# Attention and two MLPs on one core: four splits of weight sums moved into the first MLP's last block, eight moved inside their groups, ScalarE copies put behind the first product's copy

## The chip, the core and the metric

The kernel runs on one core of a Trainium2 chip. The metric is the device time of one execution in microseconds (us); lower is better. The core has a matrix engine (TensorE, PE in the profile; PEld is its loading of weights), VectorE (DVE), ScalarE (ACT), GpSimd (POOL) and SyncE (SP), which here issues all the DMA transfers. Each engine works through its own instructions in order and waits for others by semaphores. Matmuls write to PSUM banks; a bank that is read by DVE or ACT can be written again only when the read is done.

## What is computed

Windowed attention with a linear bias, then a first MLP (2304 tokens, 512 to 2048 to 512), then a second, gated MLP (512 to 1536 to 512) on normed input. In full float32; the kernel makes each float32 product of three passes over a "high" part and a "low" part (x = high + low, both in the matrix engine's reduced float32 format): high*high, high*low, low*high.

```python
def _moe_ref(x, w_in, w_out):
    h = x @ w_in
    relu6 = np.clip(h + 3.0, 0.0, 6.0)
    g = h * relu6 / 6.0
    return (g @ w_out).astype(np.float32)

def _moe2_ref(x, w_gate, w_val, w_out, rms_g):
    rms = np.sqrt(np.mean(x * x, axis=-1, keepdims=True) + 1e-06)
    xn = x / rms * rms_g
    g = xn @ w_gate
    silu = g * (1.0 / (1.0 + np.exp(-g)))
    val = xn @ w_val
    return (silu * val @ w_out).astype(np.float32)

def reference(**kwargs):            # attention, then both MLPs on [tokens, 512]
    ...
    x = _moe_ref(x=x, **moe_kwargs)
    return _moe2_ref(x=x, **moe2_kwargs)
```

## The kernel before

**First MLP.** It goes over blocks of 384 tokens (3 tiles of 128), 16 steps m of 128 hidden columns each. A step is `product1` (12 matmuls into the one bank `ps_h`, L577), a chain on ACT and DVE that makes the activation and its high and low part (L816 on ACT, L817 on DVE, L822 on ACT, L828 on DVE), and `product2` of the step before (9 matmuls, L590). Beside it run the attention of later blocks and the conversion of the second MLP's weights from 64-bit words. The conversion also writes, for each pair of steps, float32 sums of parts of the output weights to DRAM (`sum32`). In the last block, at 463 to 532 us, DVE scales the first pair's input (L736, step 2), makes sums of it, and ACT and DVE split them.

**Second MLP.** It runs in three pairs of blocks (768 tokens), 12 steps each, so in 36 groups i = 0 to 35, pair s = i // 12. A group makes gate and value by a Strassen-Winograd scheme: seven products of 6 matmuls each (products 0 to 6, L942) instead of eight. Three PSUM banks serve a group, the next group has three others. The order by hand is, in `group`: jobs called "start"; product 0 into `ps_1`; ACT copies it to `s1` (L950); product 1 into `ps_6`; DVE adds `s1` and `ps_6` to u[:,0] (L953), which frees `ps_6` for product 3; product 2 adds into `ps_1`, so it waits until L950 has read that bank; ACT makes the first silu (L956); jobs "silu"; product 3 into `ps_6`; DVE adds `s1` and `ps_6` to u[:,1] (L959), which frees `ps_6` for product 5; jobs "sum"; product 4 into `ps_5`; DVE adds (L962), which frees `ps_5` for product 6; product 5; DVE adds (L964); second silu (L965); jobs "silu 2"; product 6; DVE adds and multiplies (L968, L969); jobs "end".

For s = 0 the output product is `outputs`, every second group, from 36 matmuls (L992) whose results DVE adds up (L999). For s = 1 and 2 it is made in rounds of four groups, again by a Winograd scheme: class `Round` with seven units (c, g, a, b, e, f, d) of two halves each, whose 6 matmuls (L1116) run behind the groups i0 + 5, i0 + 6 and i0 + 7 (`phase`). DVE adds their results up (L1147), or ACT copies the first (L1145). The seven operands of a round (B22, B11, B21, T3, T1, T2, T4, halves 0 and 1) are made by jobs: "sum" is a DVE difference (L1090), "high" an ACT copy (L1093), "low" a DVE subtraction (L1096). `ROUND_JOBS` says where: the key (-1, "start") is the start of group i0 + 3, (0, "start") that of group i0 + 4, and so on; numbers stand for the positions in `phase` or `outputs`. The first round starts at group 12, so its (0, ...) jobs lie in group 16, and those of the later rounds in 20, 24, 28 and 32; the last round has its own list, `FINAL_JOBS`.

**Splits of the weights' sums.** The rounds read four of the seven weight operands from sums that must be split into high and low part first: 12 splits, `load_sum` (one DMA of 256 KB from `sum32` into the tile `ws`) and `split_sum` (ACT copies the high part, L320; DVE subtracts, L321; two DMAs store them). `SPLIT_AT` puts split k's load at the start of one group and the split itself behind the first silu ("silu") of the next; the twelve lie in groups 7, 8, 9, 10 and 12 to 19. In the order on DVE that is ahead of L959.

**Input of a pair.** `turn(s)` lays out the jobs for the next pair's input: a load of 1.5 MB (`x.load`), scaling, sums (L742 to L748), high parts (L766) and low parts (L770) of the seven Winograd operands.

Of the kernel before, what the change touches and what calls it, by code (L numbers as in the profile page):

```python
# [10 lines left out]
F32 = mybir.dt.float32  # L11
# [9 lines left out]
P = 128  # L21
# [3 lines left out]
DM = H * D  # L25
# [44 lines left out]
ADDED_TO = {"c": "C12", "a": "V", "g": "C22", "b": "C11", "e": "V", "f": "V", "d": "Z"}  # L70
SUMMED = ["C11", "C12", "C22", "V", "Z"]
BLOCK_RING = (12, 10, 11)
SPLIT_AT = (7, 8, 9, 10, 12, 13, 14, 15, 16, 17, 18, 19)
OPERANDS = "B22 B11 B21 T3 T1 T2 T4".split()
CHAINED = {"b": "a", "d": "e"}
ROUND_JOBS = {
# [2 lines left out]
    (-1, 2): [("high", "B11", 0)],  # L79
    (-1, 3): [("low", "B11", 0)],  # L80
    (-1, 4): [("sum", "T1", 0)],
    (-1, 5): [("sum", "T3", 0), ("high", "T3", 0)],
    (0, "start"): [("high", "B11", 1), ("high", "B22", 1), ("sum", "T2", 0)],
    (0, "silu"): [("low", "B11", 1), ("sum", "T1", 1), ("low", "B22", 1)],
    (0, "silu 2"): [("sum", "T3", 1), ("high", "T3", 1)],
    (0, "end"): [("low", "T3", 0)],
    (1, "start"): [("sum", "T2", 1), ("high", "B21", 0), ("high", "B21", 1)],
    (1, "silu"): [("low", "T3", 1), ("low", "B21", 0)],
    (1, "silu 2"): [("low", "B21", 1)],
    (1, "end"): [("sum", "T4", 0)],  # L90
    (1, 0): [("sum", "T4", 1)],
    (1, 2): [("high", "T1", 0), ("high", "T1", 1)],
    (1, 3): [("low", "T1", 0)],
    (2, "start"): [("low", "T1", 1), ("high", "T2", 0), ("high", "T2", 1)],
    (2, "silu"): [("low", "T2", 0), ("low", "T2", 1)],
    (2, 3): [("high", "T4", 0), ("high", "T4", 1)],
    (3, "start"): [("low", "T4", 0), ("low", "T4", 1)],
# [36 lines left out]
def fused_kernel(ctx: ExitStack, tc: tile.TileContext, qd, kd, v, w1, w2, rms_g, out, out_t):  # L134
# [113 lines left out]
    class Second:  # L248
# [57 lines left out]
                    self.x = []  # L306
                    self.begin()

        def load_sum(self, i):
            k = i % 2  # L310
            if k not in self.late:
                self.late[k] = tuple(
                    ypool.tile([P, DM], F32, tag=tag, name=name, bufs=1 if tag == "yt" else 3)
                    for tag, name in (("y", "ws"), ("yt" if k else "y", "wt"))
                )
            sp.dma_start(out=self.late[k][0], in_=self.sum32[i // 2][:, k])
# [460 lines left out]
    for p, (b, m0, m1) in enumerate(PARTS):  # L777
# [14 lines left out]
        for m in range(m0, m1):  # L792
# [68 lines left out]
            if last:  # L861
                if m == 1:
                    fed = Inputs(0)
                    fed.load()
                elif m == 2:
                    for c in range(KC):
                        fed.scale(c, vec)
                for x in early:
                    k = m - EARLY[x.m]
                    if k == 0:  # L870
                        x.load()
                    elif k == 1:
                        x.sums()
                    if k in (3, 4):
                        x.high(k - 3)
                    if k in (4, 5):
                        x.low(k - 4)
                if m == M1 - 1:
                    x.low(1)
                    parts[4].load()  # L880
                if m in FIRST_SUMS:
                    fed.sum(FIRST_SUMS[m], vec, temps.tile([P, 2, 3 * P], F32, tag="r", name="sum"))
                if m in FIRST_OPS:
                    fed.high(GROUP.index(FIRST_OPS[m]))
                    fed.low(GROUP.index(FIRST_OPS[m]))
# [4 lines left out]
    n = 3 * P  # L890
# [18 lines left out]
    def settle(which):  # L909

        for x in waiting:
            if which in x:
                x.pop(which)()
        waiting[:] = [x for x in waiting if x]
# [3 lines left out]
    def job(i, at, f, *args):  # L918
        jobs.setdefault((i, at), []).append((f, args))
# [5 lines left out]
    def group(i):  # L925
# [23 lines left out]
        product(0, ps_1)  # L949
        act.copy(s1, ps_1)  # L950
        settle("high")
        product(1, ps_6)
        vec.tensor_add(u[:, 0], s1, ps_6)  # L953
        settle("low")
# [88 lines left out]
    def total(name, d):  # L1043

        k = 5 * d + SUMMED.index(name)
        if k < 5:
            return words_of(SUMS[0], k, (1,))[:, 0]
        return words_of(BLOCK_RING[k - 5], 4, (1,))[:, 0] if k < 8 else left(F32)[:, k - 8]

    class Round:  # L1050
# [82 lines left out]
        def phase(self, off, by):  # L1133
            own = [(ps_out, "o2"), (ps_a, "T")], [banks[(by + 1) % 2][2], banks[(by + 1) % 2][1]]
            for j, (k, d) in enumerate(UNITS[off]):
                d = int(d)
                if k in CHAINED:
                    ps = self.ps[CHAINED[k], d]
                else:
                    p, tag = own[k in "gf"][d]  # L1140
                    ps = self.ps[k, d] = p.tile([P, 4 * P], F32, tag=tag, name="ps_y")[:, :n]
                self.unit(k, d, ps)
                to = total(ADDED_TO[k], d)
                if self.q == 0 and k not in "ef":
                    act.copy(to, ps)  # L1145
                else:
                    vec.tensor_add(to, to, ps)  # L1147
                if d:
                    i = 7 * self.r + self.order().index(k) + 3
                    if i // 7 < len(rounds):  # L1150
                        rounds[i // 7].fetch(rounds[i // 7].order()[i % 7])
                do(by, j)
                if self.q == ROUNDS - 1:
                    on = vec if self.final else pool
                    store = lambda name, rows, cols: sp.dma_start(
                        out=out_t[(2 * rows + d) * P : (2 * rows + d + 1) * P, (2 * (self.s - 1) + cols) * n : (2 * (self.s - 1) + cols + 1) * n],
                        in_=total(name, d),
                    )
                    if k == "b":
                        store("C11", 0, 0)  # L1160
                    elif k == "f":
                        for x, cols in (("C12", 1), ("C22", 1)):
                            (pool if x == "C12" else on).tensor_add(total(x, d), total(x, d), total("V", d))  # L1163
                            store(x, x == "C22", cols)
                    elif k == "d":
                        on.tensor_sub(total("Z", d), total("C22", d), total("Z", d))
                        store("Z", 1, 0)

    ROUNDS = M2 // ROUND
    rounds = [Round(s, q) for s in range(1, PAIRS2) for q in range(ROUNDS)]  # L1170
# [17 lines left out]
    def turn(s):  # L1188

        i, x = s * M2, Inputs(s + 1)  # L1190
        job(i + 5, "start", x.load)
        if s:
            for c in range(KC):
                job(i + 6, ("silu", "end")[c // 2], x.scale, c, act)
            job(i + 7, "silu", x.later, "S1", 0)
            job(i + 7, 2, x.later, "S2", 1)
            job(i + 7, 2, x.high, 0)
            job(i + 7, 4, x.low, 0)
            job(i + 9, 3, x.later, "S4", 2)
            job(i + 9, 3, x.high, 1)  # L1200
            job(i + 10, "silu 2", x.low, 1)
            job(i + 10, 3, x.later, "S3", 3)
            for k in range(2, 7):
                job(i + 11, {2: "silu", 3: "sum", 5: "silu 2"}.get(k, "end"), x.high, k)
                job(i + 11, {2: "silu 2", 3: "end"}.get(k, k - 3), x.low, k)
            return
        for c in range(KC):
            job(i + 6, (1, 3)[c // 2], x.scale, c, act)
# [11 lines left out]

    for x in rounds:
        x.plan(job)
    for i, at_ in enumerate(SPLIT_AT):
        job(at_ - 1, "start", W2.load_sum, i)
        job(at_, "silu", W2.split_sum, i)

    for i in range(M2 * PAIRS2):
        s, m = divmod(i, M2)
# [11 lines left out]
            outputs(i - 2, i)  # L1240
        elif i == M2 - 1:
            outputs(i - 3, i)
        if i == M2:
            for k in SEQUENCE[:3]:
                rounds[0].fetch(k)
        x = Round.all.get(i - ROUND)
# [53 lines left out]
```

## Time and profile before

| | |
|---|---|
| time, median of 3 runs | 970.88 us (969.73 to 973.53) |
| the profiled execution's own time | 970.52 us |
| its span in the profile | 968.8 us |
| time outside the span | 1.72 us |
| first MLP's last block | 463 to 532 us |
| second MLP, groups 0 to 35 | 532 to 964 us |

A page of the profile gives busy time and share of each engine. The list of waits says for how long an engine idled in front of a line, in how many places, the longest of them, and whose instruction ended it. A timeline row gives the start, the length of the run of instructions, engine, line, operation, output tile and inputs, shapes, the count, and in brackets the idle time before and what ended it. Times are microseconds from the span's start. The ends of matmuls are modelled; their starts are measured.

### The profile page before, as it was taken

The page shows a single profiled execution, that of the slowest core. Times are in us where ns is not written, and L with a number is a line of the kernel's source. Part 1 is how long each engine was busy: PE and PEld are TensorE (multiplying, and loading weights), DVE is VectorE, ACT ScalarE, POOL GpSimd, SP SyncE. Part 2 cuts the span into 40 slices and gives each one's busy share as a digit, 9 for nine tenths or more (in the row PEclk, how much of TensorE's full clock was granted, in tenths as well). Part 3 has the DMA queues.
Part 4 walks back from the last instruction along what each step waited for, and adds up shares of the span by engine and source line. Part 5 has one row for each costly group of instructions (what it writes and reads, how often), then busy time and mean ns, then how long its engine had stood idle before and what let it go on. Part 6 is the DMA issues. An engine that isn't in the chain of part 4 may idle for free.

```text
span 968.8 us, 15365 instructions
## 1 busy us (share of the span) xinstructions
PE 937.8 (97%) x5408; PEld 840.3 (87%) x5408; DVE 692.6 (71%) x1464; ACT 478.5 (49%) x1049; POOL 217.4 (22%) x359
## 2 busy tenths in 40 slices
PE   7899999999999999999999999999989998999998
PEld 4677888888888888888898999889989898999997
DVE  5788566556788778777567657787575777675778
ACT  6899556355656655654355453433135333223331
POOL 4333013233334424333323323300000000020001
PEclk9999999999999999999999999999999999999999
DMA  7546411113765555553454768775989675786626
GB/s 239 198 162 221 154 39 32 41 52 112 249 227 182 197 188 184 183 175 120 142 206 175 282 251 325 293 302 219 304 323 377 235 249 179 272 286 241 218 88 217
DMA packets 96044, 197.08 MB, mean 203 GB/s; under 512 B 7008, under 2 KB 67424, under 8 KB 92768
## 3 DMA queue, kind: packets, MB, share of 16 engines
q1 hardware_dynamic: 95968, 196.11, 58.2%
q8 instruction: 42, 0.69, 0.3%
q14 instruction: 34, 0.28, 0.1%
HBM read 142.61 MB, written 53.48 MB: 202 GB/s over the span
## 4 chain that ended last, share of the span: by engine, by line
PE 73%; DVE 11%; ACT 7%; DMA 4%; issue 3%; POOL 2%; SPq 0%; ACTq 0%; POOLq 0%; DVEq 0%
PE ps_o L590 18%; PE ps_h L577 18%; PE ps_o L942 8%; PE ps_S L942 6%; PE ps_y L1116 5%; PE ps_A L942 4%; PE ps_y L992 4%; PE ps_h L942 3%; PE ps_av L511 2%; DMA tx<-b 2%; DMA tw<-t 1%; PE ps_t L493 1%; DVE u L1147 1%; ACT t L479 1%; DVE wx L203 1%
## 5 line engine op out<-in xcount | busy, mean ns | idle before, releaser
L590 PE MATMUL ps_o<-w,g 128*128 128x512 f32 x864 | 224.1, 402 | 2.0 <-DVE w L207 1.9
L577 PE MATMUL ps_h<-xs,w 128*128 128x384 f32 x1152 | 220.4, 339 | 0.2 <-DVE t L817 0.2
L577 PEld LDWEIGHTS ps_h<-xs,w 128*128 128x128 f32 x1152 | 202.3, 188 | 6.7 <-DVE t L817 1.0
L590 PEld LDWEIGHTS ps_o<-w,g 128*128 128x128 f32 x864 | 156.1, 188 | 41.1 <-issue 6.1
L817 DVE SCALAR_TENSOR_TENSOR t<-t,ps_h 128x384 f32<-128x384 f32 x96 | 53.0, 553 | 90.5 <-ACT t L816 90.3
L816 ACT ACTIVATE t<-ps_h,three 128x384 f32<-128x384 f32 x96 | 55.3, 576 | 81.3 <-PE ps_h L577 76.0
L1116 PE MATMUL ps_y<-u 128*128 128x384 f32 x432 | 83.8, 335 | 0.2
L1163 POOL TENSOR_TENSOR u<-u 128x384 f32<-128x384 f32 x6 | 7.6, 1287 | 328.5 <-DVE u L1147 328.5
L1116 PEld LDWEIGHTS ps_y<-u 128*128 128x128 f32 x432 | 75.6, 188 | 0.8 <-DVE u L1147 0.4
L479 ACT ACTIVATE t<-t,m 128x128 f32<-128x128 f32 (+1 forms) x144 | 61.2, 426 | 29.4 <-DVE t L471 14.9
L822 ACT CAST g<-t 128x384 fp32r<-128x384 f32 x96 | 49.3, 514 | 52.5 <-DVE t L817 50.7
L965 ACT ACTIVATE r<-r 128x384 f32<-128x384 f32 x36 | 18.9, 526 | 108.3 <-DVE r L964 108.3
L828 DVE TENSOR_TENSOR g<-t,g 128x384 fp32r<-128x384 f32 x96 | 54.8, 571 | 23.1 <-ACT g L822 22.8
L942 PE MATMUL ps_o<-S,tw 128*128 128x384 f32 x336 | 66.7, 340 | 0.3 <-DVE t L962 0.3
L481 POOL TENSOR_SCALAR r<-den 128x2 f32<-128x2 f32 x72 | 27.4, 381 | 172.6 <-ACT t L479 171.0
L942 PEld LDWEIGHTS ps_o<-S,tw 128*128 128x128 f32 x336 | 59.0, 188 | 2.4 <-DVE u L953 1.6
L482 POOL TENSOR_TENSOR r<-r,minus 128x2 f32<-128x2 f32 x72 | 55.9, 776 | 6.0
L500 POOL TENSOR_SCALAR_AFFINE_SELECT pt<-pt 128x256 f32<-128x256 f32 x82 | 36.9, 452 | 81.9 <-ACT pt L498 79.0
L992 PE MATMUL ps_y<-wo,g 128*128 128x512 f32 x216 | 50.3, 391 | 0.0
L1093 ACT CAST u<-u 128x384 fp32r<-128x384 f32 x66 | 31.8, 512 | 36.6 <-DVE u L1090 20.8
L992 PEld LDWEIGHTS ps_y<-wo,g 128*128 128x128 f32 x216 | 40.8, 189 | 8.1
L464 DVE CUSTOM_DVE_ANT_0 t<-ps_s,rel 128x256 f32<-128x256 f32 (+2 forms) x128 | 45.2, 394 | 3.2 <-PE ps_s L450 3.2
(168 smaller groups left out, 1753.7 us busy)
## 6 DMA issues: line engine op xcount, KB each, us to landing
tw<-t SPq DMA_DIRECT2D x52, 896.0 KB, 6.5
wraw<-w SPq DMA_DIRECT2D x36, 512.0 KB, 4.1
wraw<-w SPq DMA_DIRECT2D x16, 1024.0 KB, 8.8
u<-s SPq DMA_DIRECT2D x48, 256.0 KB, 5.9
t<-th SPq DMA_DIRECT2D x12, 896.0 KB, 4.5
t<-tl SPq DMA_DIRECT2D x12, 896.0 KB, 4.4
u<-w SPq DMA_DIRECT2D x36, 256.0 KB, 5.3
w<-w SPq DMA_DIRECT2D x12, 512.0 KB, 2.9
```

Of the source, the lines that this page charges most:

```text
L464: vec.tensor_tensor_reduce(out=self.t[:, a, c0:], in0=s[:, c0:], in1=(rel_split if self.i in SPLITS else rel)[:, c0:], scale=2.0 ** (-8.0 ...
L479: act.activation(p, p, AF.Exp, bias=self.m[:, a : a + 1], scale=-1.0, accum_out=self.den[:, a : a + 1])
L482: pool.tensor_tensor(self.r, self.r, minus, ALU.pow)
L577: pe.matmul(ps[:, : n * P], lhsT=w[:, a, c * P : (c + 1) * P], rhs=xs[c][:, b, : n * P], start=(k == 0), stop=(k == 3 * KC - 1),)
L590: pe.matmul(o, lhsT=g[:, a, i * P : (i + 1) * P], rhs=w[:, b], start=(m == first and a == 0 and b == 0), stop=(m == last and a == 1),)
L816: act.activation(r[:, :nq], ps[:, :nq], AF.Relu, bias=three)
L817: vec.scalar_tensor_tensor(out=r[:, :nq], in0=r[:, :nq], scalar=6.0, in1=ps[:, :nq], op0=ALU.min, op1=ALU.mult)
L822: act.copy(g[:, 0, :nq], r[:, :nq])
L828: vec.tensor_sub(g[:, 1, :nq], r[:, :nq], f32(g[:, 0, :nq]))
L942: pe.matmul(ps, lhsT=w[a][:, k, c * P : (c + 1) * P], rhs=x[:, b, c], start=(start and j == 0), stop=(j == 5), skip_group_check=True,)
L992: pe.matmul(ps, lhsT=gs[i + k][:, a, t // 3, t % 3 * P : (t % 3 + 1) * P], rhs=wo[i + k][:, b], start=(k == 0 and a == 0 and b == 0), stop ...
L1116: pe.matmul(ps, lhsT=w[:, p, a, d * P : (d + 1) * P], rhs=self.part(name, p, b), start=(p == j == 0 and k not in CHAINED), stop=(p == 1 an ...
```

## The change

Four of the twelve splits (0 to 3) are made in steps 0 to 6 of the first MLP's last block, in rooms (tags "A22" and "S3") that the pair's operands use later in that block: load at step 0, 0, 3, 4 and split at the end of step 2, 3, 5, 6. The eight others go to groups 9 and 10 ("silu"), 12 ("silu 2"), 13 ("silu"), 16, 19, 20 and 21 ("sum", which is behind L959). A new position "copied" lies behind the copy of `s1`; the high parts that stood at "start" of the rounds' groups (0), (1) and (2), and the high part of T3, half 0, that stood at the end of the round phase before, go there. For the third pair the input's load is issued at the start of group 14 instead of 17; the low part of operand 1 goes from "silu 2" of group 22 to position 1 of the phase behind that group, and that of operand 6 from position 3 of the phase behind group 23 to "sum" of group 24. The first round's first three weights are fetched behind group 15 instead of 12. The end of `phase` becomes a method `give` with the same sums and stores on the same engines.

```diff
-SPLIT_AT = (7, 8, 9, 10, 12, 13, 14, 15, 16, 17, 18, 19)
+EARLY_SPLITS = {0: ("A22", 0, 2), 1: ("S3", 0, 3), 2: ("A22", 3, 5), 3: ("S3", 4, 6)}
+SPLIT_AT = {4: (9, "silu"), 5: (10, "silu"), 6: (12, "silu 2"), 7: (13, "silu"), 8: (16, "sum"), 9: (19, "sum"), 10: (20, "sum"), 11: (21, "sum")}
...
-    (-1, 5): [("sum", "T3", 0), ("high", "T3", 0)],
-    (0, "start"): [("high", "B11", 1), ("high", "B22", 1), ("sum", "T2", 0)],
+    (-1, 5): [("sum", "T3", 0)],
+    (0, "start"): [("sum", "T2", 0)],
+    (0, "copied"): [("high", "T3", 0), ("high", "B11", 1), ("high", "B22", 1)],
...
-    (1, "start"): [("sum", "T2", 1), ("high", "B21", 0), ("high", "B21", 1)],
+    (1, "start"): [("sum", "T2", 1)],
+    (1, "copied"): [("high", "B21", 0), ("high", "B21", 1)],
...
-    (2, "start"): [("low", "T1", 1), ("high", "T2", 0), ("high", "T2", 1)],
+    (2, "start"): [("low", "T1", 1)],
+    (2, "copied"): [("high", "T2", 0), ("high", "T2", 1)],
...
-        def load_sum(self, i):
+        def load_sum(self, i, tag=None):
             k = i % 2
-            if k not in self.late:
+            if tag:
+                t = opool.tile([P, 3, DM], F32, tag=tag, name="ws")
+                self.late[k] = t[:, 0], t[:, 1]
+            elif i - 2 in EARLY_SPLITS or k not in self.late:
...
+                for i, (tag, load_at, split_at) in EARLY_SPLITS.items():
+                    if m == load_at:
+                        W2.load_sum(i, tag)
+                    if m == split_at:
+                        W2.split_sum(i)
                 if m == M1 - 1:
...
         act.copy(s1, ps_1)
         settle("high")
+        do(i, "copied")
         product(1, ps_6)
...
-        job(i + 5, "start", x.load)
+        job(i + (2 if s else 5), "start", x.load)
...
-            job(i + 10, "silu 2", x.low, 1)
+            job(i + 10, 1, x.low, 1)
...
-                job(i + 11, {2: "silu 2", 3: "end"}.get(k, k - 3), x.low, k)
+                job(i + 11 + (k == 6), {2: "silu 2", 3: "end", 6: "sum"}.get(k, k - 3), x.low, k)
...
-    for i, at_ in enumerate(SPLIT_AT):
-        job(at_ - 1, "start", W2.load_sum, i)
-        job(at_, "silu", W2.split_sum, i)
+    for i, at_ in SPLIT_AT.items():
+        job(at_[0] - 1, "start", W2.load_sum, i)
+        job(*at_, W2.split_sum, i)
...
-        if i == M2:
+        if i == M2 + 3:
             for k in SEQUENCE[:3]:
                 rounds[0].fetch(k)
```

## Rows read from the trace of the kernel before

**Rows 1.** The page, part 1: busy us, share of the span, instructions.

```profile
PE 937.8 (97%) x5408; PEld 840.3 (87%) x5408; DVE 692.6 (71%) x1464; ACT 478.5 (49%) x1049; POOL 217.4 (22%) x359
```

**Rows 2.** PE's waits, whole span: us in total, times, longest us.

```profile
PE ps_h L942 <- ACT s L950: 7.3, 5, 3.1
...
PE ps_A L942 <- DVE u L959: 2.7, 5, 2.0
...
PE ps_o L942 <- DVE u L959: 2.0, 4, 1.0
...
PE ps_y L1116 <- DVE u L1147: 0.4, 1, 0.4
```

**Rows 3.** Timeline of PE in group 24: products 1 to 4.

```profile
808.22 1.22 PE L942 MATMUL ps_A<-S,tw 128*128 128x384 f32 x6
812.52 1.83 PE L942 MATMUL ps_h<-A,tw 128*128 128x384 f32 x6 [3.09 <-ACT s L950]
814.16 2.12 PE L942 MATMUL ps_A<-S,tw 128*128 128x384 f32 x6
816.08 1.42 PE L942 MATMUL ps_S<-S,tw 128*128 128x384 f32 x6
```

**Rows 4.** Timeline of ACT at the start of group 24.

```profile
810.76 0.92 ACT L1093 CAST u<-u 128x384 fp32r<-128x384 f32 x2 [6.99 <-DVE u L1090]
811.59 0.51 ACT L1093 CAST S<-u 128x384 fp32r<-128x384 f32 x1
812.00 0.47 ACT L950 COPY s<-ps_h 128x384 f32<-128x384 f32 x1
```

**Rows 5.** Timeline of DVE at the start of group 24.

```profile
807.85 0.95 DVE L770 TENSOR_TENSOR S<-sums,S 128x768 fp32r<-128x768 f32 x1
...
810.12 1.14 DVE L1090 TENSOR_TENSOR u<-u 128x384 f32<-128x384 f32 x2
812.50 0.55 DVE L953 TENSOR_TENSOR u<-s,ps_A 128x384 f32<-128x384 f32 x1 [1.24 <-ACT s L950]
```

**Rows 6.** Timeline of PE in group 8: product 5, and the outputs behind product 6.

```profile
628.19 0.63 PE L942 MATMUL ps_A<-A,th 128*128 128x384 f32 x2 [2.04 <-DVE u L959]
...
631.74 1.52 PE L992 MATMUL ps_y<-wo,g 128*128 128x512 f32 x5
```

**Rows 7.** Timeline of DVE in group 8: the split's subtraction.

```profile
626.98 0.69 DVE L321 TENSOR_TENSOR ws<-ws,wt 128x512 fp32r<-128x512 f32 x1 [2.23 <-ACT wt L320]
```

**Rows 8.** Timeline of PE in groups 14, 16, 20 and 28.

```profile
700.91 1.32 PE L942 MATMUL ps_A<-A,tw 128*128 128x384 f32 x6 [0.17 <-DVE u L959]
...
711.34 1.20 PE L942 MATMUL ps_h<-A,tw 128*128 128x384 f32 x6
712.38 1.20 PE L942 MATMUL ps_A<-S,tw 128*128 128x384 f32 x6
715.42 1.32 PE L942 MATMUL ps_h<-A,tw 128*128 128x384 f32 x6 [1.84 <-ACT s L950]
...
764.12 1.32 PE L942 MATMUL ps_h<-A,tw 128*128 128x384 f32 x6 [0.92 <-ACT s L950]
...
860.38 1.32 PE L942 MATMUL ps_h<-A,tw 128*128 128x384 f32 x6 [1.31 <-ACT s L950]
```

**Rows 9.** Timeline of DVE in groups 16 and 28: the differences ahead of L953.

```profile
713.08 1.14 DVE L1090 TENSOR_TENSOR u<-u 128x384 f32<-128x384 f32 x2
...
857.62 2.19 DVE L1090 TENSOR_TENSOR u<-u 128x384 f32<-128x384 f32 x2
```

**Rows 10.** Timeline of DVE in the first MLP's last block, steps 2 and 3.

```profile
476.61 3.17 DVE L736 TENSOR_SCALAR x2raw<-x2raw,g_sb 128x768 f32<-128x768 f32 x4
479.70 0.54 DVE L817 SCALAR_TENSOR_TENSOR t<-t,ps_h 128x384 f32<-128x384 f32 x1
```

**Rows 11.** Timeline of PE in the same block: product 1 of step 4.

```profile
480.87 2.35 PE L577 MATMUL ps_h<-xs,w 128*128 128x384 f32 x12
```

**Rows 12.** The tile `ws` (loads, ACT copies' inputs, stores of the splits): its transfers' landing.

```profile
DMA to landing us min/median/max: 2.1/6.3/11.3
```

More of the change, by code (lines that the diff above doesn't have):

```diff
@@ L1152, in phase, with give, store, combine @@
                 do(by, j)
[L1153 to L1167, printed above, removed]
+                if self.q == ROUNDS - 1 and k in "bfd":
+                    self.give(k, d)
+        def give(self, k, d):
+            def store(name, rows, cols):
+                row, col = (2 * rows + d) * P, (2 * (self.s - 1) + cols) * n
+                sp.dma_start(out=out_t[row : row + P, col : col + n], in_=total(name, d))
+            def combine(name):
+                x, on = total(name, d), vec if self.final and name != "C12" else pool
+                if name == "Z":
+                    on.tensor_sub(x, total("C22", d), x)
+                else:
+                    on.tensor_add(x, x, total("V", d))
+                store(name, name != "C12", name != "Z")
+            if k == "b":
+                store("C11", 0, 0)
+            for name in {"b": (), "f": ("C12", "C22"), "d": ("Z",)}[k]:
+                combine(name)
     ROUNDS = M2 // ROUND
```

## The prediction

> **What bounds the kernel now.** I read the busy shares first: TensorE (PE) is busy 937.8 of the span, VectorE (DVE) 71% [rows 1]. So time can only come out of PE's pauses, and the list of PE's waits says who ends them [rows 2]. The large entries of the second MLP are two. Product 2 waits for `s1` (L950, on ScalarE, ACT): 7.3 us in 5 waits. Product 5 waits for L959, the DVE sum that frees `ps_6`: 2.7 and 2.0 us in 9 waits.
>
> An idle figure is less than what a pause costs. In group 16 products 0 and 1 start at 711.34 and 712.38, so six matmuls take about 1.05; product 2 starts at 715.42, 1.99 late, where the row says 1.84 idle, since the end of product 1 is modelled 0.15 behind its pace; product 2 itself shows 1.32 instead of 1.20 [rows 8]. So I price each pause at **its idle figure plus 0.27**.
>
> A long pause costs more. In group 24 product 2 waits 3.09, and the two products that begin behind it take 1.64 and 1.92 from start to start instead of 1.05 [rows 3]: 1.5 more. In group 8 the 12 matmuls from 628.19 to 631.74 take 3.55 instead of 2.10, also 1.5 more, behind a pause of 2.04 [rows 6]. I saw PE at about half its pace nowhere else in the second MLP.
>
> **Why those waits exist.** Engines work in program order. In group 24, `do(i, "start")` puts three ACT copies (810.76 to 812.1) ahead of the copy of `s1` at 812.00 [rows 4]; the first needs a DVE difference that ends DVE's backlog at 811.26 [rows 5]. PE had the input of `s1` ready at 808.2, so nothing but the order holds it. In group 8, the split's subtraction (L321) stands on DVE ahead of L959, and DVE idles 2.23 until ACT has made that split's copy [rows 7].
>
> **The change part by part.**
> *Splits.* The subtraction no longer stands ahead of L959 in groups 7, 8, 14, 15, 18 and, below what the list names, 17 (split gone), 12 (now behind the second silu), 16 and 19 (now behind L959). Of the nine L959 waits I attribute one to group 13, which keeps its split; it is an ordinary one, as that of group 14, 0.17 [rows 8]. Eight go: 4.7 - 0.2 = 4.5 idle, plus 8 x 0.27 = 2.2, plus the slow stretch of group 8, 1.5: **8.2 us**. Group 15 keeps two low parts on DVE ahead of L959, of which one waits for its copy; I leave 0.3 there: 7.9.
> Bounds: nothing is left of 8.2 at best. At worst the subtraction that now stands ahead of L962 in groups 16, 19, 20, 21 stops product 6: L959 can start when product 3 ends and takes about 0.6, the subtraction about 0.7 [rows 7], L962 about 0.55: 1.85, against 2.1 us of products 4 and 5. It fits by 0.25, so I take nothing, with 4 x 0.5 = 2 us as the bound.
>
> *Copies behind `s1`.* Four of the five `s1` waits (groups 16, 20, 24, 28) lose their cause; the fifth, of the final round, stays (its jobs are not edited): 0.16 by what the others leave of 7.3 (1.84 + 0.92 + 3.09 + 1.31 = 7.16) [rows 2, 3, 8]. Gain 7.16 + 4 x 0.27 + 1.5 = 9.7. **What is late next** is L953 on DVE, which frees `ps_6` for product 3 and still stands behind the differences of `"start"`:
> group 16: they end at 714.22, L953 (0.55) at 714.8, product 3 is due at 712.38 + 2.1 = 714.5 [rows 8, 9]: 0.3 + 0.1 is left.
> group 24: they end at 811.26, less 0.9 for the low part (the one at 807.85) that moves from the end of group 23 behind L959 [rows 5]: L953 ends at 810.95, product 3 is due at 808.22 + 2.1 = 810.3: 0.7 is left. That low part (0.95) then stands ahead of L962, where only 0.25 was free: 0.5 more.
> group 28: two differences take 2.19 there, to 859.81 [rows 9]; L953 ends at 860.4, product 3 is due at about 860.38 - 1.31 - 0.15 + 1.05 = 859.97 [rows 8]: 0.4 + 0.1 is left.
> group 20: I leave nothing; its pause was the shortest of the four, 0.92 [rows 8].
> Together 2.1 is left: **7.6 us**. The copies now lie between `s1` and the first silu: 0.5 + 3 x 0.45 = 1.85 [rows 4] in the 2.1 that products 1 and 2 take, so the silu is not late. Bounds: 9.7 at best; at worst, if each L953 came as late as `s1` did, nothing but the second slow stretch (1.5).
>
> *One low part from ahead of the second product sums of group 22 into its round:* it stands before the running sums (L1147), for which PE waited 0.4 once [rows 2]: 0.4 + 0.27, **0.6 us**.
>
> *Four splits in the first MLP's last block.* Each adds a load, an ACT copy (0.61), a subtraction (0.69 alone) and two stores. PE has no pause there to lose, but block 2 is full on DVE: four scalings take 3.17 up to 479.78 and L817 follows at once, at 479.70 to 480.24; the next product into `ps_h` starts at 480.87 and needs it [rows 10, 11]. Pushed by 0.7, L817 ends at 480.95: 0.1 late, plus 0.1. The other three slots have DVE gaps. I take **-0.4**, with 0 and 1.5 as bounds (each of the four pushes the next L817 by a whole 0.69 and half of it shows).
> The Trainium skill, SBUF — State Buffer, section "Who interferes with whom", speaks against this place: a DVE instruction with two SBUF inputs and a GpSimd instruction that reads SBUF exclude each other, one blocking until the other is done. The differences of group 28, made beside GpSimd's output sums, agree: 2.19 for two where group 16 has 1.14 [rows 9]. By that rule a subtraction beside GpSimd's sums in blocks 2 and 3 would take some 1.3, an estimate by this ratio, L817 would end at 481.6, and the sum would be worse by about 0.6.
>
> *Other moves.* The loading of the third pair's input goes from group 17 to 14, the first round's fetch from 12 to 15: SP issues them, and PE waits for no transfer in the list [rows 2], so nothing. If that cover went, it would be as in the slower rival below. `give` issues the same sums and stores in the same order.
>
> **Sum.** 7.9 + 7.6 + 0.6 - 0.4 = 15.7 us off 970.52, the profiled execution (its span and 1.72 around it): 954.8. The median of the runs shown lies 0.36 above that execution, so **955.2**.
>
> **Rivals.**
> 1. *DVE takes ACT's place.* If L953 and L962 are later than worked out, two thirds of the copies' gain go (5 us) and the 2 us of the splits' bound: 962. For it: DVE is the next busiest engine, 71% over the whole span [rows 1], and the copies wait for its differences. Against it: even in group 24 DVE sat idle for 1.24 before L953 [rows 5]. From 959 to 966.
> 2. *The change does not do what it says:* the pauses move to the next wait of the same group and the order only changes names; only the slow stretches go (3 us at most): 968 to 971. Against it: no DVE work but that named above stands ahead of L953.
> 3. *Slower: late loads stop ACT and DVE.* In groups 16, 19, 20, 21 ACT's copy of a split waits for a load issued at the start of the group before, now behind the third pair's input; the second silu is queued behind it on ACT, and behind the subtraction on DVE L962, which product 6 needs. The copy comes some 12 us after the issue (a group and half of the next); transfers of this tile landed after 11.3 at the longest, 6.3 in the middle [rows 12]. From 12 us on every microsecond late stops PE for one, plus 1.5 of slow pace. To end above 975.7, 20.5 must be lost: four loads that land some 16 us after their issue (4 late each, and 1.5 of slow pace behind each: 22 lost, 977).
> 4. *Better:* what I left behind L953 does not show and smaller waits for ACT, below what the list names, go too: 951.
>
> **How the numbers follow.** Forecast (951.5 to 959): 0.62. Rival 1: 0.21. Rival 2: 0.06. Rival 3: 0.03. Rival 4: 0.08. The range runs from rival 4's middle over the forecast into rival 1: 950.5 to 964. A measurement of this kernel tells about 0.5% (4.9 us) from no change; faster by more means below 966: 0.62 + 0.21 + 0.08 = 0.91, less 0.01 for the edge of rival 1: 0.90; within it 0.07; slower 0.03.
>
> **What would show it.** In the profile after: no PE wait for ACT's `s1` over 0.3 but that of the final round; L959 waits gone but group 13's and perhaps 15's; no PE row at half pace behind 532; new small waits of product 3 on L953 in groups 16, 24 and 28, none above 0.7; product 6 in group 24 waits on L962; the last block as long as before within 0.6. Wrong it would be made by a wait for a load on ACT at L320, by pauses above 2 us anywhere, or by a longer last block.

## The result, and the profile after

The changed kernel takes 958.48 us (957.22 to 959.16, 4 runs). The kernel before, on the same chip, takes 971.38 (969.73 to 973.53, 4 runs). The ratio is 0.9864, 95% interval 0.9842 to 0.9887: 12.9 us faster by the medians, where 15.7 were forecast. The profiled execution took 958.45, its span is 955.6. In the code after, L942 has become L954, L950 L962, L953 L966, L959 L972, L962 L975, L577 L584, L817 L824, L321 L328, L1090 L1103 and L1093 L1106.

First the page, part 1, of after (engine, busy us, share of the span, instructions; compare [rows 1]):

```profile
PE 931.4 (97%) x5408; PEld 837.6 (88%) x5408; DVE 691.3 (72%) x1464; ACT 478.9 (50%) x1049; POOL 218.8 (23%) x359
```

The same number of instructions runs on every engine. PE's busy time fell by 6.4 us: matmuls behind a pause are counted as longer. About half of the fall lies in groups 8 and 24 (1.8 and 1.4 us), where the slow stretches of [rows 3, 6] were.

PE's waits in after, from the list for the whole span (total us, times, longest; compare [rows 2]):

```profile
PE ps_h L584 <- DVE t L824: 2.0, 2, 1.7
...
PE ps_A L954 <- DVE u L972: 0.7, 1, 0.7
PE ps_A L954 <- DVE u L966: 0.6, 2, 0.4
...
PE ps_o L954 <- DVE u L972: 0.2, 1, 0.2
```

Of the 7.3 us of waits for ACT's `s1` no entry is left, and the waits of product 3 that follow them (L966) are none above 0.4. The 4.7 us of waits for the DVE sum that frees `ps_6` are down to 0.9. What grew is the entry of the first MLP's product that waits for the activation chain (L584 for L824): 2.0 us in two waits, both in the last block. In before there is one of 0.2, in an earlier block, and none in the last.

To account for the time I took, from both traces, when each product of the second MLP begins, and by how much that is later than the usual pace of the matmuls ahead of it ("lateness": the cost of a pause with all that follows it). The stretches:

| | before | after | measured gain | forecast |
|---|---|---|---|---|
| splits off L959: groups 7, 8, 12, 14 to 19 | | | 8.4 | 7.9 |
| copies behind `s1`: groups 16, 18, 20, 24, 28, 30, 32, 34 | | | 8.2 | 7.6 |
| low part of group 22 | 0.77 | 0.47 | 0.3 | 0.6 |
| the other groups | | | -0.1 | 0 |
| second MLP, group 0 to the last matmul | 432.23 | 415.46 | 16.8 | 16.1 |
| first MLP's last block, first product to group 0 | 68.59 | 70.93 | -2.3 | -0.4 |
| start of that block | 463.31 | 464.50 | -1.2 | 0 |
| behind the last matmul, and outside the span | 6.39 | 7.56 | -1.2 | 0 |
| profiled executions | 970.52 | 958.45 | 12.1 | 15.7 |

The code ahead of the last block is the same in both, and in the kernels below its start lies between 463.16 and 464.60 with no relation to the edit. So I read the two lines of 1.2 us as differences from one execution to the next. The profiled execution of after spent 2.85 us outside its span, the other three of that kernel 1.7 to 1.9. By the stretches the edit's own part is +16.8 and -2.3, together 14.5; the medians lie 12.9 apart, and where the 1.6 between them lies is not shown.

**Group 24**, where most was expected of the copies. PE, DVE and ACT in after (compare [rows 3], [rows 5], [rows 4]):

```profile
800.11 1.22 PE L954 MATMUL ps_A<-S,tw 128*128 128x384 f32 x6
801.17 1.22 PE L954 MATMUL ps_h<-A,tw 128*128 128x384 f32 x6
802.81 1.32 PE L954 MATMUL ps_A<-S,tw 128*128 128x384 f32 x6 [0.43 <-DVE u L966]
```

```profile
801.15 1.14 DVE L1103 TENSOR_TENSOR u<-u 128x384 f32<-128x384 f32 x2
802.21 0.55 DVE L966 TENSOR_TENSOR u<-s,ps_A 128x384 f32<-128x384 f32 x1
```

```profile
800.36 0.48 ACT L962 COPY s<-ps_h 128x384 f32<-128x384 f32 x1 [4.70 <-PE ps_h L954]
801.73 0.93 ACT L1106 CAST u<-u 128x384 fp32r<-128x384 f32 x2 [0.89 <-DVE u L1103]
```

ACT now copies `s1` as soon as PE has made it, and product 2 starts 1.06 behind product 1 instead of 4.30 [rows 3]. What is late next is what was named: the two differences (L1103) hold L966 until 802.21, and product 3 starts 0.59 late and loses 0.70 with the slower matmul behind it. Group 24 went from 4.98 us of lateness to 0.96.

**Group 28** kept more than forecast: 1.49 us against 0.5. PE, DVE and GpSimd there:

```profile
848.22 1.33 PE L954 MATMUL ps_A<-S,tw 128*128 128x384 f32 x6 [0.21 <-DVE u L966]
...
851.26 1.32 PE L954 MATMUL ps_A<-A,tw 128*128 128x384 f32 x6 [0.66 <-DVE u L972]
```

```profile
845.51 2.19 DVE L1103 TENSOR_TENSOR u<-u 128x384 f32<-128x384 f32 x2
847.62 0.54 DVE L966 TENSOR_TENSOR u<-s,ps_A 128x384 f32<-128x384 f32 x1
848.09 0.89 DVE L1109 TENSOR_TENSOR u<-u,S 128x384 fp32r<-128x384 f32 x1
849.01 1.26 DVE L1103 TENSOR_TENSOR u<-u 128x384 f32<-128x384 f32 x1
```

```profile
842.39 4.90 POOL L1180 TENSOR_TENSOR u<-u 128x384 f32<-128x384 f32 x4 [213.36 <-DVE u L1160]
847.24 2.62 POOL L1178 TENSOR_TENSOR u<-u 128x384 f32<-128x384 f32 x2
```

While GpSimd makes the output's sums, DVE's subtractions take 0.81 to 1.26 instead of 0.55. Product 3 is late by 0.50 as worked out, and product 5 by another 0.94, which was not.

**The first MLP's last block** is where the rest was lost. SyncE's issues around 480 us, first of before, then of after (two rows of `x2` cover two issues and the wait between them):

```profile
477.17 0.52 SPq L634 DMA_DIRECT2D x<-yt  x1
...
481.81 5.15 SPq L634 DMA_DIRECT2D x<-yt  x2
```

```profile
478.06 4.41 SPq L330 DMA_DIRECT2D s<-ws  x2
482.57 0.53 SPq L641 DMA_DIRECT2D x<-yt  x1
...
484.17 1.04 SPq L330 DMA_DIRECT2D s<-ws  x2
...
485.93 0.72 SPq L641 DMA_DIRECT2D x<-yt  x1
...
492.33 0.52 SPq L641 DMA_DIRECT2D x<-yt  x1
```

And DVE, ACT and PE of after (compare [rows 10, 11]):

```profile
480.89 1.23 DVE L328 TENSOR_TENSOR ws<-ws 128x512 fp32r<-128x512 f32 x1
482.04 0.54 DVE L824 SCALAR_TENSOR_TENSOR t<-t,ps_h 128x384 f32<-128x384 f32 x1
...
492.82 0.56 DVE L824 SCALAR_TENSOR_TENSOR t<-t,ps_h 128x384 f32<-128x384 f32 x1 [3.85 <-ACT t L823]
```

```profile
485.31 0.59 ACT L639 COPY yt<-ps_x 128x512 f32<-128x512 f32 x1 [1.66 <-DMA x<-yt]
485.79 0.59 ACT L823 ACTIVATE t<-ps_h,three 128x384 f32<-128x384 f32 x1
...
491.72 0.59 ACT L639 COPY yt<-ps_x 128x512 f32<-128x512 f32 x1 [3.26 <-DMA x<-yt]
492.20 0.59 ACT L823 ACTIVATE t<-ps_h,three 128x384 f32<-128x384 f32 x1
```

```profile
482.64 2.37 PE L584 MATMUL ps_h<-xs,w 128*128 128x384 f32 x12 [0.33 <-DVE t L824]
...
493.43 1.84 PE L584 MATMUL ps_h<-xs,w 128*128 128x384 f32 x9 [1.70 <-DVE t L824]
```

The first wait (0.33) is the one the prediction worked out: L824 stands behind the split's subtraction. The second is a chain through a queue. SyncE reaches the split's two stores (L330) at 478.06. The second of them needs the subtraction, which ends at 482.12, so the norm's store (L641) behind it is issued at 482.57, 4 us behind the end of its copy (478.52). In before it went at 477.17, in a block that began 1.2 us earlier, and at once. The norm's tile `yt` has one buffer, so ACT's next copy into it (L639) waits 1.66 us for that store to land, and the one after that 3.26 us. The activation L823 is behind L639 on ACT, L824 waits for it on DVE, and PE waits for L824: 1.70 idle, 1.87 late.

The 3.26 us, which PE feels, are not a late issue again: the second store was issued at 485.93, as soon as its copy had ended. It was long in landing. The norm's three stores from issue to landing, in before and then in after:

```profile
DMA to landing us min/median/max: 2.5/2.6/2.6
```

```profile
DMA to landing us min/median/max: 2.6/2.6/5.7
```

Ahead of the second store the held queue had let go a load of the weights' conversion, the next split's two stores and a load, from 483.50 to 485.32; they landed between 488.94 and 490.92, and the norm's store at 491.62. ACT was ready for its copy at 488.46. With a landing of 2.6 us the tile would have been free at about 488.5, an estimate, and the wait would be gone. So SyncE's queue does harm twice: one store is issued late, and the next one lands behind the transfers ahead of it.

### The profile page after: what moved, and what is told of

Its sections match the earlier page's. It is cut to its first block, busy times and chain, and to the rows that moved or that the text cites. A ratio compares the mean times of both kernels' runs of the same rounds, so it can differ in the third digit from the quotient of the medians.

```text
span 955.6 us, 15371 instructions
## 1 busy us (share of the span) xinstructions
PE 931.4 (97%) x5408; PEld 837.6 (88%) x5408; DVE 691.3 (72%) x1464; ACT 478.9 (50%) x1049; POOL 218.8 (23%) x359
## 4 chain that ended last, share of the span: by engine, by line
PE 80%; DVE 10%; ACT 5%; issue 2%; DMA 1%; POOL 1%; SPq 0%; ACTq 0%; DVEq 0%; POOLq 0%
PE ps_o L597 18%; PE ps_h L584 17%; PE ps_o L954 9%; PE ps_S L954 7%; PE ps_y L1129 6%; PE ps_A L954 6%; PE ps_y L1005 5%; PE ps_h L954 3%; PE ps_av L518 3%; PE ps_t L500 2%; PE ps_s L457 1%; DVE u L1160 1%; DVE wx L207 1%; PE ps_s L448 1%; ACT w L209 1%
## 5 line engine op out<-in xcount | busy, mean ns | idle before, releaser
L584 PE MATMUL ps_h<-xs,w 128*128 128x384 f32 x1152 | 220.4, 339 | 2.0 <-DVE t L824 2.0
L584 PEld LDWEIGHTS ps_h<-xs,w 128*128 128x128 f32 x1152 | 202.0, 188 | 8.8 <-DVE t L824 3.3
L824 DVE SCALAR_TENSOR_TENSOR t<-t,ps_h 128x384 f32<-128x384 f32 x96 | 53.0, 553 | 91.5 <-ACT t L823 91.1
L823 ACT ACTIVATE t<-ps_h,three 128x384 f32<-128x384 f32 x96 | 55.5, 578 | 76.1 <-PE ps_h L584 70.3
L954 PE MATMUL ps_o<-S,tw 128*128 128x384 f32 x336 | 66.6, 340 | 0.3 <-DVE t L975 0.3
L954 PEld LDWEIGHTS ps_o<-S,tw 128*128 128x128 f32 x336 | 58.9, 188 | 2.4 <-DVE u L966 1.6
L207 DVE SCALAR_TENSOR_TENSOR wx<-wx,wy 128x512 uint32<-128x512 uint32 (+1 forms) x52 | 45.6, 877 | 0.0
```

What stands on the lines that cost most here:

```text
L207: vec.scalar_tensor_tensor(out=xi, in0=xi, scalar=3, in1=y, op0=ALU.logical_shift_left, op1=ALU.bitwise_or)
L584: pe.matmul(ps[:, : n * P], lhsT=w[:, a, c * P : (c + 1) * P], rhs=xs[c][:, b, : n * P], start=(k == 0), stop=(k == 3 * KC - 1),)
L823: act.activation(r[:, :nq], ps[:, :nq], AF.Relu, bias=three)
L824: vec.scalar_tensor_tensor(out=r[:, :nq], in0=r[:, :nq], scalar=6.0, in1=ps[:, :nq], op0=ALU.min, op1=ALU.mult)
L954: pe.matmul(ps, lhsT=w[a][:, k, c * P : (c + 1) * P], rhs=x[:, b, c], start=(start and j == 0), stop=(j == 5), skip_group_check=True,)
```

## The experiments

**Each half alone.** `early_alone` is the kernel before with only the four splits of the last block, the others where they were:

```diff
-SPLIT_AT = (7, 8, 9, 10, 12, 13, 14, 15, 16, 17, 18, 19)
+EARLY_SPLITS = {0: ("A22", 0, 2), 1: ("S3", 0, 3), 2: ("A22", 3, 5), 3: ("S3", 4, 6)}
+SPLIT_AT = {4: 12, 5: 13, 6: 14, 7: 15, 8: 16, 9: 17, 10: 18, 11: 19}
```

> The kernel before with splits 0 to 3 alone moved into the first MLP's last block; splits 4 to 11 and all copies stay where they were. My theory (the gain is the sum of pauses that the order on ACT and DVE made): group 7's and group 8's pauses at product 5 go (0.6 + 3.85 us), group 9 keeps its pause of product 3, group 10 loses 0.3, and the last block gets about 2.3 us longer as in the changed kernel (70.9 instead of 68.6 us from its first product to group 0). Groups 12 to 35 stay as before. Time about 971.4 - 4.7 + 2.3 = 969. Rival (the gain comes from relieving the transfers between groups 7 and 11, not from the order): parts that wait for loads elsewhere also get shorter and groups 8 to 11 lose more than 5 us together.

It took 969.9 us, ratio 0.9981 (0.9969 to 0.9994). Groups 7, 8 and 10 lost their pauses (0.79 to 0.20, 3.97 to 0.14 and 0.52 to 0.23 of lateness) and groups 12 to 34 stayed as before: the second MLP gained 3.6 us. The last block took 71.08 us, 2.5 more, with the same two waits as in after. So the four early splits give back about half of the 4.7 us that they win there, and the loss in the last block comes with them alone. Another 1.0 us went in the last group, in a wait for DVE at the output. I can't attribute it; the same place lost 0.57 and 1.09 us in two executions of the changed kernel.

`copied_alone` is the kernel before with only the copies moved:

```diff
-    (0, "start"): [("high", "B11", 1), ("high", "B22", 1), ("sum", "T2", 0)],
+    (0, "start"): [("sum", "T2", 0)],
+    (0, "copied"): [("high", "T3", 0), ("high", "B11", 1), ("high", "B22", 1)],
...
+        do(i, "copied")
```

> The kernel before with the high parts of the rounds alone put behind the copy of s1; all splits, loads and low parts stay. My theory: the pauses of product 2 in groups 16, 20, 24, 28, 30, 32 and 34 go, and product 3 waits for DVE instead, 0.4 us in group 16, 0.7 to 1.3 in group 24 (the low part of operand 6 still stands ahead there), 0.5 in group 28. About 8 us less than before: 963.5. No stretch of PE at half pace in group 24, one still in group 8. Rival (DVE takes ACT's place): product 3 waits about as long as product 2 did and only the half-pace stretch goes: 968 to 970.

It took 962.8, ratio 0.9913 (0.9898 to 0.9928): 8.6 us by the medians. Group 24 kept 1.65 of lateness, group 16 0.94, 20 0.05, 28 1.48; the last block took 68.56, as in before. The two halves, 1.5 and 8.6, don't add up to 12.9. By the length of the second MLP they gain 3.6 and 8.5 of the 16.8. The other 4.7 are splits 4 to 11, which neither moves (groups 12 and 14 to 19: 3.9), the low parts of groups 22 and 24 (0.3 and 0.7) and the 1.0 of the last group, less 1.2 that both halves gain in group 8. Splits 4 to 11 have no run of their own; their share is read from the product starts.

**One split alone.** `one_split` is the kernel before with the split of group 8 behind the second silu:

```diff
-        job(at_, "silu", W2.split_sum, i)
+        job(at_, "silu 2" if i == 1 else "silu", W2.split_sum, i)
```

> The kernel before with one edit: the split that ran in group 8 at the first rotation's first half (split 1) is put behind the second rotation's. If the pause of that group comes from where the split stands on VectorE and ScalarE, its 3.9 us of lateness falls to under 0.3 us, nothing else in the second MLP changes, and the time is about 967.5 us. If it comes from loads that land late there, the pause stays, and the time is 971.

It took 969.07, ratio 0.9978 (0.9967 to 0.9989). The pause in front of product 5 is gone. That alone does not exclude a late load, which would do no harm behind the second silu either; the trace of before does. The split's load was issued at 614.53 and landed 8.7 us later, at 623.26. ACT made the copy (L320) at 626.34, right behind a copy of the weights' conversion (L347) that had itself waited:

```profile
625.38 1.05 ACT L347 CAST th<-tx 128x1024 fp32r<-128x1024 f32 x1 [0.81 <-POOL tx L340]
626.34 0.61 ACT L320 CAST wt<-ws 128x512 fp32r<-128x512 f32 x1
```

So the order was the cause. Only 2.4 us of the 3.9 arrive in the second MLP's length, though. DVE's work is still there. Two of group 8's output matmuls now wait for it, 0.7 of lateness, and in group 9 L953 stands at the end of its backlog, where product 3 is late by 1.30 instead of 0.42. DVE and PE of this kernel in group 9:

```profile
639.75 0.95 DVE L748 TENSOR_TENSOR sums<-x2raw,sums 128x768 f32<-128x768 f32 x1
640.62 0.54 DVE L953 TENSOR_TENSOR u<-s,ps_o 128x384 f32<-128x384 f32 x1
```

```profile
641.22 0.61 PE L942 MATMUL ps_o<-S,th 128*128 128x384 f32 x2 [1.03 <-DVE u L953]
```

**The last block: queue or port?** Two kernels keep everything of after and break the chain at different links. The queue theory (the norm's store behind the split's stores on SyncE, and one buffer of `yt`) says both get back the second wait; the rival (DVE, stretched by GpSimd's sums, carries the delay) says neither does. `two_yt` gives the second and third norm tile of the last block rooms of their own:

```diff
-                yt = ypool.tile([P, KC, P], F32, tag="yt", name="yt", bufs=1)
+                if k and self.b == len(BLOCKS) - 2:
+                    yt = opool.tile([P, 3, DM], F32, tag=("A12", "S4")[k - 1], name="yt")[:, 0].rearrange("p (c q) -> p c q", c=KC)
+                else:
+                    yt = ypool.tile([P, KC, P], F32, tag="yt", name="yt", bufs=1)
```

> The changed kernel, but in the first MLP's last block the second and the third tile that carries the normed rows to DRAM has a room of its own, so that ACT's copy into it does not wait until the transfer before has landed. Queue theory (SP issues the norm's store late because it stands behind the split's stores, which wait for DVE; ACT's next copy waits for that landing, and the activation behind it on ACT comes late): the pause of 1.87 us at step 6 goes, the last block takes 69.0 to 69.3 us instead of 70.9, time about 956.7. Port theory (the split's subtraction on DVE beside GpSimd's sums is stretched from 0.69 to 1.23 us and pushes DVE's chain): the last block stays above 70.4 and the time at 958.4.

It took 954.64, ratio 0.9830 (0.9815 to 0.9844), and the last block 68.99. SyncE and ACT:

```profile
476.71 4.41 SPq L330 DMA_DIRECT2D s<-ws  x2
481.23 0.54 SPq L644 DMA_DIRECT2D x<-yt  x1
```

```profile
482.21 0.58 ACT L642 COPY yt<-ps_x 128x512 f32<-128x512 f32 x1
...
486.27 0.58 ACT L642 COPY yt<-ps_x 128x512 f32<-128x512 f32 x1
```

SyncE waits for the subtraction as long as in after (4.41), but nobody needs the store: ACT's copies into `yt` (now L642) wait for nothing. Of the two waits the first, 0.33, stays, as the queue theory has it.

`store_first` issues each early split at the start of the next step, behind the norm's store:

```diff
+            for i, (tag, load_at, split_at) in EARLY_SPLITS.items() if last else ():
+                if m == split_at + 1:
+                    W2.split_sum(i)
...
-                    if m == split_at:
-                        W2.split_sum(i)
```

> The changed kernel, but each early split is issued at the start of the next step, behind that step's store of normed rows, so the split's stores stand behind the norm's store on SP. Queue theory: the norm's store is issued about 5 us earlier in step 3, ACT's waits of 1.66 and 3.26 us for its landing shrink to under 0.5, the last block takes under 69.6 us. The pause of 0.5 at step 4 may stay, since the subtraction is still on DVE ahead of the activation's sum. Port theory: the last block stays above 70.4 us, because the subtraction still runs beside GpSimd's sums.

It took 955.33, ratio 0.9839 (0.9823 to 0.9856), and the last block 69.15; the norm's store goes at 477.64 instead of 482.57, and again only the pause of 0.33 is left. One part of the expectation missed: of ACT's two waits the first is gone, but the second is 1.27, not under 0.5.

```profile
488.25 0.59 ACT L639 COPY yt<-ps_x 128x512 f32<-128x512 f32 x1 [1.27 <-DMA x<-yt]
```

The store that it waits for was issued at 484.11 and landed 4.04 us later, behind other transfers again, so not all of the long landing in after comes from the hold. How it divides between the hold and the added transfers is not shown; so short a wait stops PE nowhere. Two different repairs of the same chain give back 1.8 to 1.9 us of the block's 2.3, with the subtraction still at 1.22 to 1.23 us beside GpSimd's sums. The queue is the cause, by SyncE's order and by the landings behind it, and not the stretched subtraction.

`later_splits` was meant as a third repair, with the splits four to five steps later (its expectation speaks of the same four steps, the edit does not keep to them):

```diff
-EARLY_SPLITS = {0: ("A22", 0, 2), 1: ("S3", 0, 3), 2: ("A22", 3, 5), 3: ("S3", 4, 6)}
+EARLY_SPLITS = {0: ("A22", 0, 6), 1: ("S3", 0, 7), 2: ("A22", 8, 10), 3: ("S3", 8, 11)}
```

> The changed kernel with its four early splits moved later inside the same four steps of the last block, so that the norm's store stands ahead of each pair of split stores on SyncE. The queue theory: the two waits of the first MLP's products for their rotated operand (2.0 us together in the changed kernel) go, the last block from its first product to the first product of the second MLP takes 68.6 to 68.9 us where the changed kernel took 70.93, and the time is about 956 us. The port theory (the subtractions on VectorE are stretched by GpSimd's sums, and VectorE carries the delay): the waits stay, 70.9 us, about 958.5 us.

I missed: 961.2, ratio 0.9899 (0.9883 to 0.9915), last block 75.84. The waits at 482 and 493 are gone, as the queue theory said, but there is a worse one at the block's end. ACT, PE, and the windows there (busy us of each engine, then granted clock as a share of full speed, DMA share, GB/s):

```profile
526.56 0.83 ACT L773 CAST S<-sum 128x768 fp32r<-128x768 f32 x1 [4.78 <-DMA s<-ws]
```

```profile
529.00 4.21 PE L584 MATMUL ps_h<-xs,w 128*128 128x384 f32 x12 [3.90 <-DVE t L824]
```

```profile
529.00:532.00 3.00, 3.00 (x9) 3.00 (x10) 2.29 (x3) 1.22 (x2) 0.07 (x1) 0.50 0.09 38
```

The early splits borrow the rooms A22 and S3, in which the second MLP's first operands are made at the end of the block. ACT's copy into S3 (L773) waits 4.78 us until the last split is stored. So the splits may not be late either: their place is bounded on one side by the norm's store and on the other by the rooms.

**What stretches DVE in group 28.** `no_pool_sums` is after with GpSimd's sums of the second pair left out; C12, C22 and Z of that pair's output lack the added term:

```diff
             def combine(name):
...
-                if name == "Z":
+                if not self.final:
+                    pass
+                elif name == "Z":
```

> The changed kernel without the sums that GpSimd makes of every output group but the last (the sums of two products that go into the output quadrants are left out for those, so part of the output is missing). Theory that GpSimd's sums stretch VectorE's work in group 28: the pair of L1103 that took 2.16 us there takes 1.1 us, the pauses of 0.50 and 0.94 us on L966 and L972 shrink to under 0.2 us each, and the time falls by about 1.3 us to 957. Theory that the pauses come from the order on VectorE alone: both pauses stay, no change, 958.5 us.

It took 956.59, ratio 0.9849 (0.9833 to 0.9866). DVE and PE in group 28:

```profile
845.90 1.15 DVE L1103 TENSOR_TENSOR u<-u 128x384 f32<-128x384 f32 x2
847.61 0.56 DVE L966 TENSOR_TENSOR u<-s,ps_A 128x384 f32<-128x384 f32 x1 [0.57 <-PE ps_A L954]
848.09 0.55 DVE L1109 TENSOR_TENSOR u<-u,S 128x384 fp32r<-128x384 f32 x1
848.67 0.56 DVE L1103 TENSOR_TENSOR u<-u 128x384 f32<-128x384 f32 x1
```

```profile
848.40 1.22 PE L954 MATMUL ps_A<-S,tw 128*128 128x384 f32 x6
...
850.51 1.22 PE L954 MATMUL ps_A<-A,tw 128*128 128x384 f32 x6
```

The same instructions in the same order take 1.15, 0.55 and 0.56 where they took 2.19, 0.89 and 1.26. Both pauses are gone, and of the group's 1.49 of lateness 0.09 is left. GpSimd's work beside DVE costs group 28 1.4 us, not DVE's order.

**Towards a better kernel.** `best` moved the early splits as in `later_splits`, splits 5 and 7 to the sums' place, and two kinds of jobs behind the second silu: the difference that opens the rounds' groups (0), that is 16, 20, 24, 28 and 32, and a sum that opens group 9:

```diff
-SPLIT_AT = {4: (9, "silu"), 5: (10, "silu"), 6: (12, "silu 2"), 7: (13, "silu"), 8: (16, "sum"), 9: (19, "sum"), 10: (20, "sum"), 11: (21, "sum")}
+SPLIT_AT = {4: (9, "silu"), 5: (10, "sum"), 6: (12, "silu 2"), 7: (13, "sum"), 8: (16, "sum"), 9: (19, "sum"), 10: (20, "sum"), 11: (21, "sum")}
...
-    (0, "start"): [("sum", "T2", 0)],
-    (0, "silu 2"): [("sum", "T3", 1), ("high", "T3", 1)],
+    (0, "silu 2"): [("sum", "T3", 1), ("high", "T3", 1), ("sum", "T2", 0)],
...
-        job(i + 9, "start", x.later, "S4", 2)
+        job(i + 9, "silu 2", x.later, "S4", 2)
```

> The changed kernel with the early splits behind the norm's stores, splits 5 and 7 put at the sums' place of groups 10 and 13, and the sums and differences that opened groups 0 and 9 put behind their second rotation. By the pauses left in the changed kernel's trace: last block -2.0 us, groups 10 and 13 -0.75, groups 9, 16, 24 and 28 up to -2.0: about 953 us. If the port between VectorE and GpSimd sets what is left, only the last block gains: 956 us.

It took 962.04, ratio 0.9905 (0.9890 to 0.9920): not better. Its last block ends as that of `later_splits` (74.95), and its second MLP took 415.98, 0.5 more than in after. Groups 13 and 28 gained 0.43 and 0.3; group 10 changed only the place of its pause; groups 17, 21, 29 and 33 lost 0.35 each to the moved jobs.

What was right in it went into a last pair on one chip: the changed kernel once more, and `two_yt` with split 7 at (13, "sum").

> The changed kernel, unedited, beside the next one. Its last block should take 70.9 us from its first product to the first product of the second MLP, with two waits of 2.0 us together for the rotated operand, and the time should be 958.5 us; if it comes out near 955, the gain of the two repairs measured before was the spread between executions and not the last block.

> The changed kernel with rooms of their own for the second and third tile of the norm in the last block, and with split 7 moved from group 13's first rotation to its sums. Queue theory: the last block takes 69.0 us, group 13 loses its pause of 0.44 us, no other group changes, and the time is 2.3 us under that of the unedited changed kernel run beside it, about 956.2. If instead the first MLP's earlier end only moves the waits into the second MLP, both times agree within 0.5 us.

The changed kernel took 958.11 (957.17 to 959.86), ratio 0.9867 (0.9846 to 0.9888), the other 955.29 (954.45 to 955.45), 0.9834 (0.9815 to 0.9854). No two runs of the two overlap, and the gain of the repairs is not the spread between executions: the medians lie 2.8 us apart, where 2.3 were expected. In the profiled executions the last block took 71.57 and 68.92 us, and group 13's lateness fell from 0.51 to 0.08. With the waits for the norm gone and split 7 moved the change is worth about 16 us.

## Why the prediction was right, and where it was not

The sign and the mechanism of the second MLP are right: the waits that were named went, for the reason that was given. 12.9 us came where 15.7 were forecast, and 958.48 lies in the forecast's own range of 951.5 to 959, but only 0.5 under its end. The second MLP brought 0.7 more than forecast and the last block 1.9 less; that they partly cancel is luck.

- **Splits off L959**, 7.9 forecast, 8.4 measured. The pauses in front of product 5 in groups 7, 8, 12, 14 and 16 to 19 went, the slow stretch behind group 8's too, and what was to stay in groups 13 and 15 stayed (0.44 and 0.21). The four splits that now stand ahead of the sum that frees `ps_5` (L975) in groups 16, 19, 20 and 21 cost nothing, as worked out. One reading was wrong without changing the sum: the nine listed waits stood in groups 7, 8, 12 to 16, 18 and 19, so 12, 16 and 19 were not "below what the list names"; 19's was the longest of the odd groups, 1.03.
- **Copies behind `s1`**, 7.6 forecast, 8.2 measured. The remainders behind L966 came out as worked out: 0.39 in group 16 (0.4), 0.70 in group 24 (0.7), 0.50 in group 28 (0.5), 0.05 in group 20 (0). The moved low part was to cost 0.5 at product 6 of group 24 and cost 0.2. Two slips nearly cancel. The fifth `s1` wait was put down as one of the final round that stays, since "its jobs are not edited". It stood in group 34, whose copies of T2 belong to the round before and are edited, and 0.39 went; so did smaller waits in groups 18, 30 and 32, 0.6 together. And in group 28 DVE was followed to L966 and not on to L972: 0.94 of lateness there.
- **Low part of group 22**, 0.6 forecast, 0.3 measured. The price was right (0.36 idle, 0.64 late), but the wait did not go, it shrank: the running sum still stands behind the group's own product on DVE, and 0.36 of lateness with 0.08 idle is left.
- **The early splits**, -0.4 forecast, -2.3 measured, beyond the bound of 1.5. This is the step that failed. Its DVE part was nearly right: L824 was pushed, and PE was late by 0.49 at 482.64, against 0.2. What was not followed is SyncE. The text priced the load, the copy, the subtraction "and two stores" by what they take on ACT and DVE, and named transfers only as landing times; it did not ask what is queued behind the stores on SyncE. There the norm's store was queued. It went 4 us late, the next one took 5.7 us to land instead of 2.6 behind the transfers issued ahead of it, and through the single buffer of `yt` that stopped ACT, then DVE, then PE for 1.87. No wait of before showed it, because in before nothing stood ahead of that store.
- **The clause "PE waits for no transfer in the list"** was used to price SyncE's moved loads at nothing. For the loads it held. As an argument it fails: the list names the last releaser only, and in after, too, it says DVE L824 where a store two engines further back is the cause.

The Trainium skill, SBUF — State Buffer, "Who interferes with whom", was cited for a subtraction that would take some 1.3 us beside GpSimd's sums. It took 1.23 (the next split's, at 484.03 with GpSimd idle, 0.68). In group 28 taking GpSimd's sums away shows that they are what stretches such subtractions: 2.19 against 1.15 for two. By that rule the sum was to be 0.6 worse. The wait that it names cost 0.49, 0.3 more than forecast. The rule was right about DVE, and it did not decide the block.

Of the rivals, the first (DVE takes ACT's place) is seen beyond what was worked out only in group 28, and there it is GpSimd's doing. The second did not occur: the lateness went and did not move to the next wait. The slower one did not occur either: no copy of a split waits for its load on ACT in the second MLP. Of the better one a part came, the 0.6 us of smaller waits.

## What to carry to other kernels

When work with stores is moved, follow the issuing queue as an engine of its own: which wait does the moved store bring to the head of the queue, what stands behind it, and whose only buffer does that free? A store issued ahead of its data held all later ones here, for 4 us, and the next tile's store landed behind them; issue it behind those whose data is ready, or give the tile behind it a second buffer. And borrowed rooms give a moved job a last date as well as a first.

## What the hardware did that I had not expected

The half pace behind long pauses is the granted clock (0.58 in group 24 of before, from 812.5 to 816.3), and the length of the pause alone does not decide it. Windows of group 8 behind its pause, in before (pause 2.04 idle) and in `copied_alone` (2.35 idle), columns as above:

```profile
628.00:631.70 3.70, 3.51 (x12) 3.51 (x13) 1.25 (x3) 1.06 (x2) 0.00 (x0) 0.61 0.33 123
```

```profile
629.30:631.50 2.20, 2.20 (x12) 2.20 (x13) 1.11 (x2) 0.27 (x1) 0.00 (x0) 1.00 0.45 168
```

The same twelve matmuls take 3.5 us in the one and 2.2 in the other, at a clock of 0.61 (part of the stretch at 1.2 GHz) and 1.00 (2.4 GHz), though the second pause was longer. That accounts for the 1.2 us by which group 8 was less late in `copied_alone` (2.74 against 3.97), which that edit does not touch. What decides between the two stays open. Behind the pause of 1.70 at 493 in after the clock stayed at 1.00; behind the 3.90 in `later_splits` it was 0.50.
